# Casting v in its loading DMA, a PSUM bank for each pair of heads, and a new order: one core of Trainium2

## The chip, the cores and the metric

The kernel runs on one core of one Trainium2 chip. The metric is the device time of one execution in microseconds, taken as the median of several runs. A profile of one execution shows, for each instruction, its start and duration.

Names of the engines in the profile: PE is the matrix engine (PEld its weight loads), DVE the vector engine, ACT the scalar engine, POOL the GpSimd engine, SP the sync engine, which here only issues DMAs.

## The reference

The first half is linear attention with phi(x) = elu(x) + 1, over 8 batches, 8 heads, 576 positions and 64 values for each head. The second half is a multiplicative feed-forward network on the 4608 x 512 result.

```python
def phi(x):
    return np.where(x > 0, x, np.exp(x) - 1.0) + 1.0
q_p, k_p = phi(q), phi(k)
kv = einsum('bhsd,bhse->bhde', k_p, v)
z = sum(k_p, axis=2)
num = einsum('bhsd,bhde->bhse', q_p, kv)
den = einsum('bhsd,bhd->bhs', q_p, z)[..., None] + 1e-06
x = (num / den).transpose(0, 2, 1, 3).reshape(4608, 512)
a, b = x @ w1, x @ w2            # 512 x 1024 each
out = ((a * b) @ w3) @ w_out     # 1024 x 1024, then 1024 x 512
```

All inputs and the output are f32 in memory. The kernel computes its matmuls in bf16 and accumulates in f32.

## The kernel before, in words

The work is written as small steps. A string, `ORDER`, lists every step by name and arguments, and the program calls them in that order. Each engine executes its own instructions in the order in which the string issues them, and waits with semaphores for what it reads. So the order within one engine is fixed by hand, and only the waits between engines are left to run time. A second string, `GATES`, makes some loads wait for another load. SP and POOL issue DMAs in order, too: an issue that has to wait keeps all later ones on that engine back.

Of each batch the first 512 positions (128 partitions x 4, the index `j`) make chunk `b`. The last 64 positions of two batches share a tile (the "r" steps), and the eight remainders make chunk 8. `hp` is one of four pairs of heads.

Loading. `ld:n,b,h0,nh,queue` loads heads h0 to h0+nh of k, q or v of batch b as f32, one row of 1 KB for each head and partition; `lr` and `lp` load remainders; `lw`, `lo` and `l3` load w1 and w2, w_out and w3 with a cast to bf16 in the DMA, issued by POOL. `ld` tiles come from a pool of five buffers; a load waits until the tile five loads earlier is no longer read.

Feature map. `x` is exp on ACT, `t` is max(x, 0) + 1 on DVE, `m` the minimum of the two on DVE, which is phi; each `x` and `t` takes four heads, 1024 elements in a partition; each `m` before takes two heads, 512 elements. `xr`, `tr`, `mr` are the same for remainders.

Attention. `v` casts v into a tile `vt` with a column of ones beside each head, so that one product gives both kv and z; `vr` does so for the remainder. `kv` (batches 0 and 1) and `kk` (the others) are the products; `kc`, `kh` and `kg` copy them from PSUM to SBUF as bf16. `qt` and `qc` transpose phi(q) on PE and copy it (batches 0 and 1), `qd` does so by a DMA from SP (batches 2 to 7). `na` is phi(q) times kv for a pair of heads, `nd` the division on DVE (three instructions). `xp` and `xc` transpose the result on PE and copy it (chunks 0 to 2), `xd` does so by a DMA (chunks 3 to 7). `nar`, `ndr`, `qdr`, `xdr` are the remainder's.

Feed-forward. `w3t`, `w3c`, `wa`, `wf`, `wc` make w3 @ w_out once, so that the second half needs one product fewer. `f:c,f` gives 128 columns of a and of b for a chunk, 4 + 4 matmuls of 512 columns; it needs the transposed chunk `xt`. `ac` copies a from PSUM on ACT, `ab` multiplies it with b on DVE. `o:c,m` needs all eight `ab` of a chunk, 8 matmuls; `oc` copies the result and `st` stores it. `ol` is an `o` in two halves, the last of all. `warm` steps are matmuls on zeros.

PSUM has two pools: four buffers of one bank (`mm_ps`: w3, warm, qt, xp, a, b, o) and two of two banks (`at_ps`: wa, kv, kk, na, nar).

The lines that a sentence doesn't replace, the products of batches 0 and 1 (before):

```python
o = got(ps, ("kv", b), at_ps, [P, 2, 512], F32, "at", "kvp")
dst = o[:, g, a * PW:(a + 1) * PW]          # two pairs of heads in one bank
for j in range(NJ):
    nc.tensor.matmul(dst, kj[:, hp, j]..., vt[:, j, 2 * hp:2 * hp + 2, :]..., start=(j == 0), stop=False)
nc.tensor.matmul(dst, kr[...], vrz[...], start=False, stop=True)
```

Of the kernel before, what the change touches and what calls it, by code (L numbers as in the profile page):

```python
# [18 lines left out]
def kernel(  # L19
# [71 lines left out]


    @step
    def const(i):
        if i == 0:
            nc.vector.memset(zero, 0.0)  # L96
        elif i == 1:
            make_identity(nc, ident)
        elif i == 2:
            for t in vts:  # L100
                nc.vector.memset(t[:, :, :, D:E1], 1.0)
        elif i == 3:
            nc.vector.memset(vrz, 0.0)
            for s in range(2):
                nc.vector.memset(vrz[s * R:(s + 1) * R, s, :, D:E1], 1.0)
        else:
            nc.vector.memset(kvb[i - 4], 0.0)
# [8 lines left out]
    @step  # L116
    def ld_(n, b, h0, nh, queue):
        t = got(raw, (n, b), ld, [P, H * W], F32, "ld", f"{n}32")
        return queue_of[queue].dma_start(
            out=t[:, h0 * W:(h0 + nh) * W].rearrange("p (h x) -> p h x", x=W),  # L120
            in_=src[n][b, h0:h0 + nh, 0:NJ * P, :].rearrange("h (p j) d -> p h (j d)", j=NJ))

# [53 lines left out]
    @step  # L176
    def m(n, b, h0, hp):
        d = got(ph, (n, b), phi_p, [P, KC, NJ, 2, D], BF16, n)
        s = slice((2 * hp - h0) * W, (2 * hp - h0 + 2) * W)
        nc.vector.tensor_tensor(  # L180
            out=d[:, hp].rearrange("p j u d -> p u j d"),
            in0=ts[n, b, h0][:, s].rearrange("p (u j d) -> p u j d", u=2, j=NJ),
            in1=es[n, b, h0][:, s].rearrange("p (u j d) -> p u j d", u=2, j=NJ), op=ALU.min)
# [31 lines left out]
    @step  # L215
    def v_(b, h0, nh, eng):
        copy_of[eng](  # L217
            out=vts[b % len(vts)][:, :, h0:h0 + nh, 0:D],
            in_=raw["v", b].rearrange("p (h j d) -> p j h d", h=H, j=NJ)[:, :, h0:h0 + nh])

    @step
    def vr(b, eng):
        s = b % 2
        r = slice(s * R, (s + 1) * R)
        copy_of[eng](out=vrz[r, s, :, 0:D],
                     in_=raw["vr", b // 2][r].rearrange("p (h d) -> p h d", d=D))
# [3 lines left out]
    def kv(b, hp):  # L230
        o = got(ps, ("kv", b), at_ps, [P, 2, 512], F32, "at", "kvp")
        g, a = divmod(hp, 2)
        kj = ph["k", b]
        kr = ph["kr", b // 2, 2 if b > 1 else b]
        vt = vts[b % len(vts)]
        dst = o[:, g, a * PW:(a + 1) * PW]
        for j in range(NJ):
            nc.tensor.matmul(dst, kj[:, hp, j].rearrange("p u d -> p (u d)"),
                             vt[:, j, 2 * hp:2 * hp + 2, :].rearrange("p h e -> p (h e)"),
                             start=(j == 0), stop=False)  # L240
        nc.tensor.matmul(dst, kr[:, hp * P:(hp + 1) * P],
                         vrz[:, b % 2, 2 * hp:2 * hp + 2, :].rearrange("p h e -> p (h e)"),
                         start=False, stop=True)
# [4 lines left out]
    def kk(b, hp):  # L248
        o = got(ps, ("kk", b), at_ps, [P, 2, 512], F32, "at", "kvp")[:, 0]
        kj, kr, vt = ph["k", b], ph["kr", b // 2, 2], vts[b % len(vts)]  # L250
        for j in range(NJ + 1):
            for u in range(2):
                h = 2 * hp + u
                nc.tensor.matmul(o[u * D:(u + 1) * D, hp * E1:(hp + 1) * E1],  # L254
                                 kj[:, hp, j, u] if j < NJ else kr[:, h * D:(h + 1) * D],
                                 vt[:, j, h] if j < NJ else vrz[:, b % 2, h],
                                 start=(j == 0), stop=(j == NJ))

    @step
# [6 lines left out]
    def kc(b, g0, ng, r, eng):  # L266
        rows = slice(r * D, (r + 1) * D)
        copy_of[eng](  # L268
            out=kvb[b][rows, 2 * g0:2 * (g0 + ng), r, :].rearrange(
                "p (g a) e -> p g a e", a=2),  # L270
            in_=ps["kv", b][rows, g0:g0 + ng, 0:2 * PW].rearrange(
                "p g (a u e) -> p g a u e", a=2, u=2)[:, :, :, r, :])

    @step
    def kh(b, hp, r, eng):
        rows = slice(r * D, (r + 1) * D)
        g, a = divmod(hp, 2)
        c = a * PW + r * E1
        copy_of[eng](out=kvb[b][rows, hp, r, :], in_=ps["kv", b][rows, g, c:c + E1])

    @step
    def qt(b, h, n):
        t = ps["qt", b, h] = mm_ps.tile([P, NCH], F32, tag="mm", name="qtp").bitcast(
            BF16).rearrange("p (i t) -> p i t", t=P)
        for i in range(n):
            for j in range(NJ):
                nc.tensor.transpose(
                    t[:, i * NJ + j, :], ph["q", b][:, h + i, j].rearrange("p u d -> p (u d)"), ident)

    @step  # L290
    def qc(b, h, n, eng):
        d = got(sb, ("qt", b), att, [P, KC, NJ * P], BF16, "qt")
        copy_of[eng](out=d[:, h:h + n, :].rearrange("p i (j t) -> p (i j) t", t=P),
                     in_=ps["qt", b, h][:, 0:n * NJ, :])

    @step
    def qd(b):
        d = got(sb, ("qt", b), att, [P, KC, NJ * P], BF16, "qt")
        nc.sync.dma_start(out=d.rearrange("p c (j t) -> p (c j) t", t=P),
                          in_=ph["q", b].rearrange("p c j u d -> p (c j u d)"), transpose=True)  # L300
# [7 lines left out]
    def na(b, hp):  # L308
        o = ps["na", b, hp] = at_ps.tile([P, 2, 512], F32, tag="at", name="nd")
        for j in range(NJ):  # L310
            nc.tensor.matmul(o[:, j // 2, (j % 2) * 256:(j % 2) * 256 + PW],  # L311
                             sb["qt", b][:, hp, j * P:(j + 1) * P],
                             kvb[b][:, hp].rearrange("p u e -> p (u e)"),
                             start=True, stop=True)

    def divide(o, r, dst):
        nc.vector.tensor_scalar_add(out=r, in0=o[:, :, :, D], scalar1=1e-6)
        nc.vector.reciprocal(out=r, in_=r)  # L318
        nc.vector.tensor_tensor(  # L319
            out=dst, in0=o[:, :, :, 0:D],  # L320
# [3 lines left out]
    def nd(b, hp):  # L324
        x = got(sb, ("xn", b), att, [P, NJ, DM], BF16, "xn")
        r = small.tile([P, NJ, 2], F32, tag="r4", name="r")
        o = ps["na", b, hp].rearrange("p i (a x) -> p (i a) x", a=2)[:, :, 0:PW]
        divide(o.rearrange("p j (u e) -> p j u e", e=E1), r,
               x[:, :, hp * P:(hp + 1) * P].rearrange("p j (u e) -> p j u e", u=2))

    @step
    def nar(b):
        o = ps["nar", b] = at_ps.tile([P, 2, 512], F32, tag="at", name="ndr")
        for hp in range(KC):
            g, a = divmod(hp, 2)
            nc.tensor.matmul(o[:, g, a * PW:(a + 1) * PW], sb["qtr", b // 2][:, hp, :],  # L336
                             kvb[b][:, hp].rearrange("p u e -> p (u e)"),
# [3 lines left out]
    def ndr(b):  # L341
        x = got(sb, ("xnr", b // 2), att, [P, DM], BF16, "xnr")
        r = small.tile([P, 2, 4], F32, tag="r", name="r")
        w = slice((b % 2) * R, (b % 2 + 1) * R)
        divide(ps["nar", b][w, :, 0:2 * PW].rearrange("p g (a e) -> p g a e", e=E1), r[w],
               x[w].rearrange("p (g a e) -> p g a e", g=2, e=D))
# [93 lines left out]

    @step
    def o(c, m):
        d = ps["o", c, m] = mm_ps.tile([P, DM], F32, tag="mm", name="o_ps")
        for f in range(FC):
            nc.tensor.matmul(d, sb["ab", c][:, f, m * P:(m + 1) * P], wf_sb[:, f, :],  # L445
                             start=(f == 0), stop=(f == FC - 1))
# [32 lines left out]
    const:0 lr:k,0,s const:8 warm:26,0 warm:18,9 const:1 lr:v,0,s const:6 zr:0,1 l3:0 const:2 const:9  # L479
    l3:1 zr:0,0 const:11 l3:2 xr:k,0,0 tr:k,0,0 l3:3 const:5 lo:0,2 const:3 lo:2,2 lo:4,2 vr:0,a const:7  # L480
    w3t:0 const:10 lo:6,2 warm:8,1 w3c:0,v l3:4 mr:k,0,0 const:4 l3:5 w3t:1 warm:8,2 w3c:1,a
    ld:k,0,0,4,g w3t:2 warm:8,3 w3c:2,a ld:k,0,4,4,g w3t:3 warm:8,4 w3c:3,v ld:q,0,0,4,g wa:0,1 wa:1,1
    ld:q,0,4,4,g wa:2,1 ld:v,0,0,4,g wa:3,1 wa:4,1 ld:v,0,4,2,g wa:5,1 ld:v,0,6,2,g wa:6,1 wa:7,1 l3:6
# [106 lines left out]
```

## Time and profile before

| what | value |
|---|---|
| median of 3 runs | 251.77 us (251.26 to 253.02) |
| the profiled execution: its time | 251.52 us |
| the profiled execution: its span | 249.67 us |
| PE busy | 236.0 us |
| DVE busy | 164.1 us |
| ACT busy | 122.9 us |
| DMA | 50.10 MB, mean 201 GB/s |
| granted PE clock | 1.0 throughout |

How to read it: the span runs from the first to the last recorded event; the time of the execution holds some 1.85 us more around it. Busy times of different engines lie beside each other, so they don't add up to the span. A line of the timeline has start, duration, engine, line of the source, operation, output and inputs, shape and count, and in brackets the idle time of the engine before it with the instruction that ended it. A matmul's duration includes its way through the pipeline (about 0.16 us), so a row of eight of 512 columns shows 1.89 us although the next one can begin 1.73 us after the first.

### The profile page before, as it was taken

The numbers are of one execution on the slowest core, as the hardware profiler recorded it, in microseconds if no ns is written. First come the engines' busy times: TensorE is split into PE (matmuls) and PEld (weight loads), VectorE is DVE, ScalarE is ACT, GpSimd is POOL, SyncE is SP. The second block draws the span as 40 slices with busy tenths as digits, with TensorE's granted clock in tenths as the row PEclk, the third lists the DMA queues.
The fourth block names the chain that finished last, engine by engine and source line by source line (L and its number), as shares of the span: only waits on it lengthen the run. The fifth ranks groups of instructions, "written<-read, shape, count | busy, mean of one in ns | idle before, by whom it ended". The sixth has DMA issues, their size and how long they took to land.

```text
span 249.7 us, 4327 instructions
## 1 busy us (share of the span) xinstructions
PE 236.0 (95%) x1620; PEld 122.9 (49%) x1636; DVE 164.1 (66%) x364; ACT 122.9 (49%) x190; POOL 36.4 (15%) x59
## 2 busy tenths in 40 slices
PE   6897889979999989999999999999999999999994
PEld 6654844445444555454444454544544444444442
DVE  7518764977868999959649889786775365042320
ACT  3409554776956774665744835153352332323211
POOL 8554720001100210011000032200001100000000
PEclk9999999999999999999999999999999999999999
DMA  6999999999998999999999699975409511210155
GB/s 120 204 265 348 214 198 294 314 248 319 336 240 227 281 294 287 211 248 351 189 265 335 182 248 260 291 175 107 105 12 128 179 22 21 91 38 29 55 144 153
DMA packets 69621, 50.10 MB, mean 201 GB/s; under 512 B 41312, under 2 KB 64096, under 8 KB 69600
## 3 DMA queue, kind: packets, MB, share of 16 engines
q1 hardware_dynamic: 60416, 31.86, 54.1%
q0 software_dynamic: 9040, 17.83, 28.0%
q8 instruction: 13, 0.21, 0.3%
q10 hardware_dynamic: 144, 0.13, 0.2%
q14 instruction: 8, 0.07, 0.1%
HBM read 38.80 MB, written 9.44 MB: 193 GB/s over the span
## 4 chain that ended last, share of the span: by engine, by line
PE 56%; DMA 32%; DVE 4%; issue 3%; ACT 2%; POOL 1%; SPq 0%; ACTq 0%; POOLq 0%; DVEq 0%
PE a_ps L420 17%; PE o_ps L445 17%; PE b_ps L420 17%; DMA v<-in_v_dram 13%; DMA q<-in_q_dram 9%; DMA w_sb<-in_moe_w_dram 4%; DMA wo<-in_moe_w_out_dram 3%; DMA k<-in_k_dram 3%; DVE xn L319 2%; PE nd L311 2%; PE kvp L254 1%; POOL w3b L159 1%; PE ndr L336 1%; PE o_ps L472 1%; ACT vt L217 1%
## 5 line engine op out<-in xcount | busy, mean ns | idle before, releaser
L420 PEld LDWEIGHTS <-w_sb 128*128 128x128 bf16 x576 | 55.6, 98 | 64.6 <-issue 0.6
L439 DVE TENSOR_TENSOR ab<-a_sb,b_ps 128x512 bf16<-128x512 f32 x72 | 49.0, 684 | 43.7 <-PE b_ps L420 40.1
L434 ACT COPY a_sb<-a_ps 128x512 f32<-128x512 f32 x72 | 42.1, 584 | 58.8 <-PE a_ps L420 52.7
L420 PE MATMUL a_ps<-xt,w_sb 128*128 128x512 bf16 x256 | 66.0, 379 | 0.5 <-ACT xt L358 0.5
L420 PE MATMUL b_ps<-xt,w_sb 128*128 128x512 bf16 x256 | 66.0, 379 | 0.0
L445 PE MATMUL o_ps<-wf_sb,ab 128*128 128x512 bf16 x267 | 62.9, 379 | 1.0 <-issue 0.2
L445 PEld LDWEIGHTS <-ab 128*128 128x128 bf16 x280 | 26.4, 98 | 30.3 <-DVE ab L439 1.2
L463 POOL DMA_DIRECT2D out_dram<-o_sb x24 | 14.5, 605 | 148.7 <-ACT o_sb L451 130.9
L451 ACT COPY o_sb<-o_ps 128x512 f32<-128x512 f32 x24 | 14.0, 585 | 34.1 <-PE o_ps L445 31.9
L319 DVE TENSOR_TENSOR xn<-nd,r 128x512 bf16<-128x512 f32 x32 | 22.1, 692 | 1.1
L166 ACT ACTIVATE e<-q 128x1024 bf16<-128x1024 f32 x16 | 16.5, 1056 | 1.8 <-DMA q<-in_q_dram 1.8
L166 ACT ACTIVATE e<-k 128x1024 bf16<-128x1024 f32 x16 | 16.4, 1058 | 0.9 <-DMA k<-in_k_dram 0.8
L451 DVE COPY o_sb<-o_ps 128x512 f32<-128x512 f32 x11 | 7.6, 687 | 8.0 <-PE o_ps L445 8.0
L217 ACT CAST vt<-v 128x1024 bf16<-128x1024 f32 (+1 forms) x11 | 10.2, 933 | 5.4 <-PE kvp L254 2.7
L180 DVE TENSOR_TENSOR k<-t,e 128x512 bf16<-128x512 bf16 x32 | 12.2, 418 | 0.4 <-ACT e L166 0.2
L172 DVE TENSOR_SCALAR t<-q 128x1024 bf16<-128x1024 f32 x16 | 10.9, 688 | 2.1 <-DMA q<-in_q_dram 2.1
L180 DVE TENSOR_TENSOR q<-t,e 128x512 bf16<-128x512 bf16 x32 | 11.9, 420 | 0.2
L311 PE MATMUL nd<-kvb,qt 128*128 128x130 bf16 x128 | 10.9, 220 | 0.9 <-DVE kvb L268 0.4
L172 DVE TENSOR_SCALAR t<-k 128x1024 bf16<-128x1024 f32 x16 | 10.5, 688 | 1.2 <-DMA k<-in_k_dram 1.1
L311 PEld LDWEIGHTS <-qt 128*128 128x128 bf16 x128 | 8.7, 98 | 4.9 <-DVE xn L319 1.0
L113 PE MATMUL warm<-zero 128*128 128x128 bf16 x116 | 9.2, 241 | 1.2 <-DVE zero L96 1.2
L318 DVE RECIPROCAL r<-r 128x8 f32<-128x8 f32 (+1 forms) x40 | 8.1, 202 | 1.4
(76 smaller groups left out, 191.6 us busy)
## 6 DMA issues: line engine op xcount, KB each, us to landing
v<-in_v_dram SPq DMA_DIRECT2D x6, 1024.0 KB, 9.8
k<-in_k_dram SPq DMA_DIRECT2D x6, 1024.0 KB, 8.7
q<-in_q_dram SPq DMA_DIRECT2D x6, 1024.0 KB, 9.2
out_dram<-o_sb POOLq DMA_DIRECT2D x24, 256.0 KB, 6.1
w3b<-in_moe_w_dram POOLq DMA_DIRECT2D x8, 256.0 KB, 8.1
out_dram<-o_sb SPq DMA_DIRECT2D x7, 256.0 KB, 2.3
v<-in_v_dram POOLq DMA_DIRECT2D x3, 512.0 KB, 18.9
out_dram<-o_sb SPq DMA_DIRECT2D x9, 128.0 KB, 2.4
```

Source lines behind the costliest of these rows:

```text
L166: return nc.scalar.activation(out=e[:, 0:nh * W], in_=raw[n, b][:, h0 * W:(h0 + nh) * W], func=AF.Exp)
L172: nc.vector.tensor_scalar(out=d[:, 0:nh * W], in0=raw[n, b][:, h0 * W:(h0 + nh) * W], scalar1=0.0, scalar2=1.0, op0=ALU.max, op1=ALU.add)
L180: nc.vector.tensor_tensor(out=d[:, hp].rearrange("p j u d -> p u j d"), in0=ts[n, b, h0][:, s].rearrange("p (u j d) -> p u j d", u=2, j=NJ ...
L217: copy_of[eng](out=vts[b % len(vts)][:, :, h0:h0 + nh, 0:D], in_=raw["v", b].rearrange("p (h j d) -> p j h d", h=H, j=NJ)[:, :, h0:h0 + nh])
L311: nc.tensor.matmul(o[:, j // 2, (j % 2) * 256:(j % 2) * 256 + PW], sb["qt", b][:, hp, j * P:(j + 1) * P], kvb[b][:, hp].rearrange("p u e - ...
L319: nc.vector.tensor_tensor(out=dst, in0=o[:, :, :, 0:D], in1=r.unsqueeze(3).to_broadcast(list(r.shape) + [D]), op=ALU.mult)
L420: nc.tensor.matmul(o, w[:, kc, f * P:(f + 1) * P], xt_of(c)[:, :, kc, :], start=(kc == 0), stop=(kc == KC - 1))
L434: return copy_of[eng](out=d, in_=ps["a", c, f])
L439: nc.vector.tensor_mul(out=d[:, f, :], in0=sb["a", c, f], in1=ps["b", c, f])
L445: nc.tensor.matmul(d, sb["ab", c][:, f, m * P:(m + 1) * P], wf_sb[:, f, :], start=(f == 0), stop=(f == FC - 1))
L451: return copy_of[eng](out=d, in_=ps["o", c, m])
L463: queue_of[queue].dma_start(out=dst, in_=sb["o", c, m][r])
```

## The change

Four things are changed.

1. v of batches 0 and 1 (first 512 positions) is loaded by a new step `lv` on POOL, whose DMA casts to bf16. There is no `v` step for these batches. The product reads the loaded tile itself, which has no column of ones, so `kv` has for each `j` a second matmul of two columns against a small tile of ones.
2. Each pair of heads of `kv` has a PSUM bank of its own: a two-bank buffer for each two pairs. A tile of a pair is now laid out as one, head, head, one (`PW` = 130 columns), so that the two sums stand at its ends; `vt`, `vrz`, `kvb`, `na`, `nd`, `nar`, `ndr` and the copies follow this layout. For the batches 2 to 7 the cast `v` is divided by the head's place in its pair, `v:b,u`, and not by the half of the heads.
3. `m` takes four heads, 1024 elements, and phi's tile has the layout [P, NJ, H, D].
4. `ORDER` is another one, and so is the order of `GATES`. The new kernel also has the steps `kz`, `nt`, `ln`, `xm` and `o_part`; of these only `o_part` is used, by `o`. `const:12` sets the ones and two tiles that nothing reads.

```diff
+    ones = consts.tile([P, 2], BF16)
+    def of_pairs(t):
+        return t.rearrange("p j (c u) e -> p j c (u e)", u=2)
+    @step
+    def lv(b, h0, nh):
+        if ("vb", b) not in raw:
+            raw["vb", b] = ld.tile([P, H * W], F32, tag="ld", name="vb").bitcast(
+                BF16)[:, 0:H * W].rearrange("p (h j d) -> p h j d", h=H, j=NJ)
+        return nc.gpsimd.dma_start(
+            out=raw["vb", b][:, h0:h0 + nh].rearrange("p h j d -> p h (j d)"),
+            in_=v[b, h0:h0 + nh, 0:NJ * P, :].rearrange("h (p j) d -> p h (j d)", j=NJ))
     @step
-    def m(n, b, h0, hp):
-        d = got(ph, (n, b), phi_p, [P, KC, NJ, 2, D], BF16, n)
+    def m(n, b, h0, nh):
+        d = got(ph, (n, b), phi_p, [P, NJ, H, D], BF16, n)
...
     @step
-    def v_(b, h0, nh, eng):
+    def v_(b, u, eng):
         copy_of[eng](
-            out=vts[b % len(vts)][:, :, h0:h0 + nh, 0:D],
-            in_=raw["v", b].rearrange("p (h j d) -> p j h d", h=H, j=NJ)[:, :, h0:h0 + nh])
+            out=of_pairs(vts[b % len(vts)])[:, :, :, 1 + u * D:1 + (u + 1) * D],
+            in_=raw["v", b].rearrange("p (c u j d) -> p u j c d", u=2, j=NJ, d=D)[:, u])
     @step
     def kv(b, hp):
-        o = got(ps, ("kv", b), at_ps, [P, 2, 512], F32, "at", "kvp")
         g, a = divmod(hp, 2)
-        dst = o[:, g, a * PW:(a + 1) * PW]
+        dst = got(ps, ("kv", b, g), at_ps, [P, 2, 512], F32, "at", "kvp")[:, a, 0:PW]
         for j in range(NJ):
-            nc.tensor.matmul(dst, kj[:, hp, j].rearrange("p u d -> p (u d)"),
-                             vt[:, j, 2 * hp:2 * hp + 2, :].rearrange("p h e -> p (h e)"),
-                             start=(j == 0), stop=False)
+            k2 = of_pair(kj[:, j], hp)
+            nc.tensor.matmul(dst[:, 1:PW - 1].rearrange("p (u d) -> p u d", u=2), k2,
+                             vb[:, 2 * hp:2 * hp + 2, j], start=(j == 0),
+                             stop=False, skip_group_check=True)
+            nc.tensor.matmul(dst[:, 0:PW:PW - 1], k2, ones, start=False, stop=False, skip_group_check=True)
...
     def divide(o, r, dst):
-        nc.vector.tensor_scalar_add(out=r, in0=o[:, :, :, D], scalar1=1e-6)
+        nc.vector.tensor_scalar_add(out=r, in0=o[:, :, 0:PW:PW - 1], scalar1=1e-6)
...
```

The order, at the places that the prediction speaks of. First batch 0's products:

```diff
-    lw:0,1,256 x:q,0,4,4 m:q,0,0,0 warm:10,10 m:q,0,0,1 wc:4,v warm:10,11 m:k,0,4,2 qt:0,0,2 lw:1,1,256
-    v:0,0,4,v warm:10,12 t:q,0,4,4 lw:0,1,512 v:0,4,2,a kv:0,1 warm:10,13 m:q,0,4,3 lw:1,1,512 v:0,6,2,a
-    qc:0,0,2,v kv:0,2 kv:0,0 m:q,0,4,2 kh:0,2,1,a kv:0,3 kh:0,2,0,a kc:0,0,1,1,a kc:0,0,1,0,v qt:0,2,2
+    wf:5 m:q,0,0,4 lw:0,1,256 x:q,0,4,4 t:q,0,4,4 qt:0,0,2 wc:5,v warm:10,13 qc:0,0,2,a lw:1,1,256
+    m:q,0,4,4 kv:0,0 kv:0,1 lw:0,1,512 kv:0,2 kc:0,0,1,a kc:0,0,0,v kv:0,3 lw:1,1,512 kh:0,2,0,a
+    kh:0,2,1,v na:0,1 qt:0,2,2 kh:0,3,1,a kh:0,3,0,v ld:k,1,0,8,g nd:0,1 w3t:6 qc:0,2,2,a na:0,0 w3c:6,v
+    xp:0,1 w3t:7 nd:0,0 xc:0,1,a na:0,2 ld:q,1,0,8,g wf:6 lr:k,1,s w3c:7,v lv:1,0,4 lr:v,1,s nd:0,2
```

Then from chunk 1's o steps to chunk 2's f steps:

```diff
-    kk:2,1 kk:2,2 kk:2,3 v:3,0,4,v ld:q,4,0,8,s ab:1,5 o:1,1 kg:2,0,a kg:2,1,a v:3,4,4,v m:q,3,0,0
-    m:q,3,4,3 na:2,2 m:q,3,0,1 oc:1,1,a na:2,0 o:1,3 m:q,3,4,2 nd:2,0 st:1,1,g qd:3 nd:2,2 xp:2,0
-    oc:1,3,a o:1,0 t:k,3,4,4 vr:4,a st:1,3,g t:k,3,0,4 x:k,3,4,4 xp:2,2 x:k,3,0,4 na:2,3 m:k,3,4,2
-    na:2,1 m:k,3,4,3 o:1,2 nd:2,3 oc:1,0,a xc:2,2,a st:1,0,g m:k,3,0,0 xc:2,0,a nd:2,1 xp:2,3 x:q,4,0,4
-    m:k,3,0,1 xp:2,1 t:q,4,0,4 xc:2,3,a kk:3,0 kk:3,1 kk:3,2 kk:3,3 oc:1,2,v xc:2,1,a ld:v,4,0,8,s
-    kg:3,0,v st:1,2,g x:q,4,4,4 kg:3,1,v f:2,0 vr:5,v t:q,4,4,4 ac:2,0,a f:2,1 ab:2,0 ac:2,1,a m:q,4,4,2
+    x:q,3,0,4 f:1,5 ab:1,4 ld:k,4,0,8,s x:k,3,4,4 f:1,7 ac:1,5,a ab:1,5 ac:1,7,a lp:k,2,s ab:1,7 o:1,0
+    o:1,3 ld:q,4,0,8,s oc:1,0,a m:q,3,4,4 st:1,0,g m:q,3,0,4 x:k,3,0,4 t:k,3,4,4 qd:3 na:2,1 na:2,3
+    m:k,3,4,4 o:1,1 x:k,4,4,4 t:k,3,0,4 m:k,3,0,4 x:k,4,0,4 t:k,4,4,4 o:1,2 oc:1,1,a oc:1,3,v nd:2,1
+    st:1,1,g st:1,3,g oc:1,2,a t:k,4,0,4 na:2,0 xp:2,1 st:1,2,g nd:2,3 xr:k,2,2 xc:2,1,a ld:v,4,0,8,s
+    x:q,4,4,4 nd:2,0 na:2,2 xp:2,3 xc:2,3,a nd:2,2 kk:3 xp:2,0 tr:k,2,2 xp:2,2 lp:k,3,s kg:3,1,a
+    mr:k,2,2 xc:2,0,a xc:2,2,v m:k,4,0,4 f:2,1 kg:3,0,v m:k,4,4,4 ac:2,1,a t:q,4,0,4 x:q,4,0,4 f:2,4
```

SP's loads and transposes from batch 2 to the first load of batch 6, without the remainders, and the end of the order:

```diff
-    ld:v,2 ld:k,2 ld:q,2 ld:v,3 ld:q,3 qd:2 ld:k,3 ld:q,4 qd:3 ld:v,4 ld:k,4 qd:4 ld:k,5 xd:3 ld:q,5 ld:v,5 xd:4 qd:5 ld:v,6
+    ld:k,2 ld:v,2 ld:q,2 ld:v,3 ld:q,3 ld:k,3 qd:2 ld:k,4 ld:q,4 qd:3 ld:v,4 qd:4 xd:3 ld:q,5 ld:v,5 ld:k,5 ld:v,6 qd:5 xd:4
...
-    o:8,1 oc:8,3,a st:8,3,s o:8,0 oc:8,1,a st:8,1,s o:8,2 oc:8,0,v st:8,0,s o:7,0 oc:8,2,v st:8,2,s
-    oc:7,0,a st:7,0,s ol:7,3
+    st:8,2,s o:8,3 oc:8,1,v st:8,1,s o:8,0 oc:8,3,a st:8,3,s ol:7,3 oc:8,0,a st:8,0,s
```

At the start, POOL issues `l3:0` before the identity matrix is made (`const:1`); before it came after it.

## The prediction

> **What bounds the kernel now.** I read the page first (busy shares, slices), then the chain that ended last, then the timeline around each hole of PE. The page:
>
> ```profile
> PE 236.0 (95%) x1620; PEld 122.9 (49%) x1636; DVE 164.1 (66%) x364; ACT 122.9 (49%) x190; POOL 36.4 (15%) x59
> PE   6897889979999989999999999999999999999994
> DMA  6999999999998999999999699975409511210155
> ```
>
> PE is busy 95% of the span and nearly all its holes lie in the first 15 slices of 6.24 us. The DMA engines are full for about 25 slices. So only two things can pay: a shorter head, or fewer holes up to about 90 us. The chain shows who made these holes (start us, us, what):
>
> ```profile
> 32.68 19.71 DMA v<-in_v_dram
> 52.41 0.64 ACT vt L217
> ...
> 64.44 11.17 DMA q<-in_q_dram
> ...
> 76.88 7.36 DMA k<-in_k_dram
> ```
>
> The load of v of batch 1 lands at 52.41, and its cast for PE comes after that. The holes themselves, in the timeline (the bracket is the idle time before and its releaser):
>
> ```profile
> 36.36 0.38 PE L420 MATMUL a_ps<-xt,w_sb 128*128 128x512 bf16 x1 [0.45 <-ACT xt L358]
> ...
> 51.79 0.39 PE L238 MATMUL kvp<-vt,k 128*128 128x130 bf16 x4 [0.59 <-ACT vt L217]
> ...
> 53.09 0.39 PE L238 MATMUL kvp<-vt,k 128*128 128x130 bf16 x4 [0.58 <-ACT vt L217]
> ...
> 54.70 0.39 PE L238 MATMUL kvp<-vt,k 128*128 128x130 bf16 x4 [0.28 <-DVE kvb L279]
> ...
> 64.43 1.03 PE L420 MATMUL a_ps<-xt,w_sb 128*128 128x512 bf16 x4
> ...
> 79.09 1.92 PE L445 MATMUL o_ps<-wf_sb,ab 128*128 128x512 bf16 x7
> ...
> 88.70 0.40 PE L353 MATMUL xtp<-ident,xn 128*128 128x128 bf16 x4 [0.77 <-DVE xn L319]
> ...
> 89.79 1.04 PE L420 MATMUL a_ps<-xt,w_sb 128*128 128x512 bf16 x4
> ```
>
> The reader should take four marks from these: chunk 0's f steps end at about 51.0, chunk 1's begin at 64.43, chunk 1's o steps begin at 79.09, chunk 2's f steps begin at 89.79. After 89.79 PE runs to its last matmul at about 246.3 with holes of 0.5 us at most. The tail:
>
> ```profile
> 244.56 0.59 ACT L451 COPY o_sb<-o_ps 128x512 f32<-128x512 f32 x1 [4.59 <-PE o_ps L445]
> ...
> 246.35 0.37 ACT L474 COPY o_sb<-o_ps 128x256 f32<-128x256 f32 x1 [1.21 <-PE o_ps L472]
> 246.75 0.37 ACTq L476 DMA_DIRECT2D out_dram<-o_sb  x1
> ```
>
> The prices that I use, in us: f or o 8 x 0.216 = 1.73 of PE (four matmuls start 0.86 apart); one na, xp, or half a qt 0.22; kk 0.78; on DVE ab 0.69, t 0.65 (two take 1.29), nd 1.03 (60.25 to 61.29 from one to the next), xc 0.42; on ACT x 1.06, ac, oc and xc 0.59.
>
> **What the skill says.** "VectorE: DVE Perf Modes", section "The perf-mode tier table": tensor_tensor on bf16 in SBUF runs two elements a cycle, no more. The trace agrees (418 ns for 512, below one element a cycle), so the 1024-element minimum costs 418 ns plus another 512 at two a cycle, 267: 0.69 us. "DMA: Bandwidth & Descriptors", section "SWDGE vs HWDGE vs iDMA": only GpSimd's DMAs cast. Here every casting load is indeed on POOL's queue. "PSUM — Partial Sum Buffer", section "PSUM bank collisions": accesses by two engines must be kept apart by bank; the wait at 54.70, a kv behind copies from its bank, agrees. "TensorE: Matmul & The Clock Gate", section "Back-to-back issue gap": a matmul of up to 64 columns has a floor of about 25 ns; no row here has two columns.
>
> **The change, part by part.**
>
> Cast by DMA. Six casts of v go (on ACT three of 0.63 us and one of 1.04, on DVE 0.69 and 0.43). The number of POOL issues stays. The DMA view of the first 60 us, in slices of 1.5 us, has about 348 GB/s written where the f32 loads of k, q and v run (16 to 25 us), and about 200 GB/s of bf16 where casting loads run, which is 400 GB/s read: 1 MB takes 2.6 instead of 3.0 us. Two of them bring later loads 0.8 us forward, and l3:0 ahead of the identity on POOL perhaps 0.5 more.
>
> Ones matmuls. 8 kv steps x 4 = 32 more pairs of weight load and matmul. Ends: 25 ns (the skill's floor) and 57 ns (pitch of the 130-column pairs, (0.39-0.22)/3). I take 50 ns: 1.6 us of PE, 0.8 in each kv group. It is in the sums below; in batch 1 DVE is later than PE anyway, so it hides there, and costs 0.8 if DVE is not.
>
> Minimum over four heads. 64 x 0.419 becomes 32 x 0.69: 4.7 us less DVE over the span, spread out. On the critical DVE chains it counts 0.07 to 0.15 for each pair.
>
> Bank per pair. The 0.46 us wait in kv of batch 0 and the one at 54.70 go. But kv now takes both attention PSUM buffers, so na must wait for a group's copies; the order gives these first.
>
> Order. I followed the new queues engine by engine, each instruction starting at the later of its queue and its inputs.
>
> (a) Head to chunk 0's f. On DVE from 17.84 (end of wa): three copies, then t, m of k and q, bound by ACT's four exponentials between its copies, until m:q,0,4,4 ends at 27.0. The kv steps end on PE at 27.9, and na:0,1 starts there (29.60 before). DVE then has four nd, two w3c, and the xc: 28.3 + 4.1 + 1.3 + waits gives 33.9 and xt is complete at 35.4. Under it PE does both wf:6 and wf:7. Before, f work went on at 36.36 with wf:7 (1.73) still to do and 0.86 of f done, so it equals a start at 37.2. Gain 1.8. Eight f steps: 35.4 + 13.85 = 49.25, against 51.0.
>
> (b) Chunk 0's o, batch 1's attention. v1 is in by about 49.5, without cast, so no kv waits. DVE then has 15 operations and four nd in a row up to xc:1,2: t, t, m 2.0, ab and copies, m, t, m, four nd with four xc. With the waits on PE's na and on ACT it ends at about 63.0; xc:1,0 on ACT follows, and f:1,3 starts at 63.6 (64.43 before). Gain now 0.8.
>
> (c) f of chunk 1: 8 x 1.73 + kk 0.78 + one wait of 0.75 on ab:1,3 behind the minima: 79.0, against 79.09. Gain 0.1. The old order had f:1 running while DVE had less in front of ab.
>
> (d) Chunk 1's o to chunk 2's f. Here the new order queues on DVE, between ab:1,7 and f:2,1's last input xc:2,2: m:q3 twice, t and m of k3 twice, t:k4 twice, oc:1,3, four nd, tr, mr, xc. That is 4 x 0.69 + 4 x 0.65 + 0.68 + 4.12 + 3 x 0.42 = 11.4. ab:1,7 itself ends 1.3 after f:1,7 (its matmuls' tail, ab:1,5 ahead of it): 79.0 + 1.3 + 11.4 = 91.7. PE has only four o (6.92), four na, four xp and kk in the same time, 9.5. ACT is no earlier: x:q,4,4,4 sits before xc:2,3, kg:3,1 and xc:2,0, and q4, now behind k4 in SP's queue, lands at about 88.5 to 89.5; + 1.06 + 0.59 + 0.4 + 0.59 is 91 to 92. I take 91.6. The old order needed 10.7 for this stage, the new one 12.6. At the same remaining work PE stands 1.8 later than before.
>
> (e) From there to the last matmul nothing is left to win it back: PE had next to no holes. Both orders keep at least one f step (1.73) against about 1 us of DVE beside its ab. So + 1.8 there too.
>
> (f) Tail. ol's ACT copy now comes before oc:8,0 on ACT. After 246.72 + 1.8 come the issue 0.37, the copy 0.59, and two issues on SP of some 0.34, in place of the ACT issue alone: the last landing is 1.3 later.
>
> Sum: 1.8 + 1.3 = 3.1. The profiled execution took 251.52 (span 249.67 and 1.85 around it), which is 0.25 below the median of 251.77. So 251.52 + 3.1 = 254.6, 1.1% above the median. About 1% is what a measurement of this kernel can tell from no change.
>
> **Rivals.**
>
> 1. The head's gain is kept. Mechanism: DVE's chain in (d) is not the last to end; the point that decides is when f:2,1 starts: below 89.8 instead of 91.6. For it: DVE needs 4.7 us less, and v's cast and the bank waits, 2.3 us of holes from 51 to 55.3, are gone. Against it: the 11.4 us queue holds even when every load is early. Then f:2,1 starts 1.8 before the old mark (88.0), and the tail's 1.3 stays: 251.52 - 1.8 + 1.3 = 251.0, down to 249 where x:q,4 and the ones cost nothing.
>
> 2. Loads come late in the middle. q5, v5, k5 and v6 now stand behind xd:3 in SP's queue, while before k5 stood ahead of it. From v4's landing (about 97) to nd:3,1 (about 106) the DMA engines have little to do. xd:3 took 5.8, four loads at 3.75 follow, and x:q,5 sits on ACT ahead of ac:3,1. If q5 is 3.5 late, PE waits that long once its two f buffers are full: 258.1. Against it: kk:5 comes 6.8 us of PE work later than before.
>
> 3. It does not do what it says: the engines already do f32 and casting loads at one read rate, and the orders cost the same: 252.
>
> **How the numbers follow.** Forecast 0.45 (253.2 to 256.5: slower 0.35, within 1% 0.10); rival 1 0.33 (within 1% 0.23, faster 0.10); rival 2 0.17 (slower); rival 3 0.05 (within 1%). Sum: faster 0.10, within 0.38, slower 0.52. The range leaves the best of rival 1 and the worst of rival 2 out: 250.0 to 258.2.
>
> **What would show it.** Right: first f step of chunk 0 at 35 to 36, no ACT or DVE wait before the kv of batch 1, f:2,1 at 91 to 92 with idle before it from xt, DVE without idle from ab:1,7 to there, oc:8,0 after ol's copy in the tail. Wrong: f:2,1 below 90, or PE idle over 1 us behind e or a_sb after 110.

## The result, and the profile after

The changed kernel takes 255.56 us (median of 4 runs, 254.21 to 257.37), the kernel before on the same chip 252.06 (251.26 to 253.02). The ratio is 1.0142, with an interval of 1.0095 to 1.0189. The forecast was 254.6, slower by about 1.1%. The profiled execution, the shortest of the four, took 254.21 us with a span of 252.4, against 251.52 and 249.67 before: 2.7 us more. A ratio here and below is taken over the runs that lie within 1.5% of their kernel's fastest.

The page after (busy times, then PE and its granted clock in 40 slices of 6.31 us):

```profile
PE 237.8 (94%) x1668; PEld 124.6 (49%) x1668; DVE 163.8 (65%) x344; ACT 116.1 (46%) x178; POOL 34.1 (14%) x59
PE   8799899989799979999999999999999999999991
PEclk9999999999999999999999999999999999999997
```

ACT lost 6.8 us of work and DVE almost none of its sum. PE is full in every slice after the fifteenth but for the last one, which is nearly empty: the end is longer. (The lower clock in that slice lies behind PE's last matmul.) The marks of the prediction and the holes beside them, in PE's timeline after:

```profile
36.68 1.02 PE L471 MATMUL a_ps<-xt,w_sb 128*128 128x512 bf16 x4 [0.61 <-DVE xt L409]
...
54.13 1.04 PE L495 MATMUL o_ps<-wf_sb,ab 128*128 128x512 bf16 x4 [1.01 <-DVE ab L490]
...
64.31 0.40 PE L404 MATMUL xtp<-ident,xn 128*128 128x128 bf16 x4 [0.97 <-DVE xn L342]
65.43 1.02 PE L471 MATMUL a_ps<-xt,w_sb 128*128 128x512 bf16 x4 [0.72 <-ACT xt L409]
...
80.10 2.11 PE L495 MATMUL o_ps<-wf_sb,ab 128*128 128x512 bf16 x9
...
88.93 0.40 PE L334 MATMUL nd<-kvb,qt 128*128 128x130 bf16 x4 [0.86 <-DVE xn L342]
89.97 0.32 PE L282 MATMUL kvp<-vt,k 128*64 128x65 bf16 x8 [0.41 <-DVE xn L342]
91.86 1.02 PE L471 MATMUL a_ps<-xt,w_sb 128*128 128x512 bf16 x4 [0.47 <-ACT xt L409]
```

No kv of batch 1 waits for a cast any more. In place of those waits stand a hole at 54.13, two at 64 to 65 and three at 89 to 92, all behind DVE's or ACT's queue. The hole at 54.13 begins on ACT (first line; the second is the vector engine's `ab` behind it):

```profile
45.73 0.62 ACT L248 CAST vrz<-v32r 64x512 bf16<-64x512 f32 x1 [2.22 <-DMA v32r<-in_v_dram]
...
46.99 0.69 DVE L490 TENSOR_TENSOR ab<-a_sb,b_ps 128x512 bf16<-128x512 f32 x1 [2.44 <-ACT a_sb L485]
```

The new order put `vr:1`, the cast of the v remainder, on ACT. It waits 2.22 us for its load with the last four `ac` copies of chunk 0 behind it; `ab` is late, and `o` waits for `ab`. The last microseconds, all engines:

```profile
246.56 0.34 SPq L534 DMA_DIRECT2D out_dram<-o_sb  x1
247.03 0.37 ACT L532 COPY o_sb<-o_ps 128x256 f32<-128x256 f32 x1 [2.93 <-PE o_ps L530]
247.43 0.37 ACTq L534 DMA_DIRECT2D out_dram<-o_sb  x1
247.90 0.59 ACT L509 COPY o_sb<-o_ps 128x512 f32<-128x512 f32 x1 [0.49 <-ACT o_sb L532]
248.51 1.10 SPq L521 DMA_DIRECT2D out_dram<-o_sb  x2
```

`oc:8,0` (L509) now follows `ol`'s copy (L532), and two stores are issued after it. Before, the issue at 246.75 was the last event of this kind.

Busy times in stretches show where PE gained and lost (length; then PE, PEld, DVE, ACT and POOL busy with their counts, PE clock, DMA share, GB/s). Before:

```profile
52.00:66.00 14.00, 12.66 (x106) 7.53 (x105) 10.55 (x27) 10.70 (x20) 1.93 (x4) 1.00 1.12 312
80.00:92.00 12.00, 11.18 (x111) 6.12 (x111) 11.54 (x30) 8.62 (x13) 2.59 (x4) 1.00 1.12 286
92.00:247.00 155.00, 153.11 (x934) 74.48 (x941) 97.92 (x215) 65.99 (x103) 9.73 (x16) 1.00 0.68 169
```

After:

```profile
52.00:66.00 14.00, 11.30 (x99) 6.56 (x96) 11.60 (x30) 8.96 (x15) 2.20 (x4) 1.00 1.11 319
80.00:92.00 12.00, 10.27 (x107) 5.79 (x105) 11.11 (x25) 8.03 (x13) 2.23 (x4) 1.00 1.17 250
92.00:247.00 155.00, 154.95 (x952) 75.28 (x950) 99.69 (x202) 64.55 (x101) 8.73 (x16) 1.00 0.65 164
```

From 52 to 66 and from 80 to 92 PE does 2.3 us less than before; from 92 on it does 1.8 more and is full. Of these 1.8 us, 0.7 lie behind the last matmul of the kernel before, which began at 246.00.

### The profile page after: what moved, and what is told of

It reads as the page before. It is cut to its first block, busy times and chain, and to the rows that moved or that the text cites. A ratio compares the mean times of both kernels' runs of the same rounds, so it can differ in the third digit from the quotient of the medians.

```text
span 252.4 us, 4363 instructions
## 1 busy us (share of the span) xinstructions
PE 237.8 (94%) x1668; PEld 124.6 (49%) x1668; DVE 163.8 (65%) x344; ACT 116.1 (46%) x178; POOL 34.1 (14%) x59
## 4 chain that ended last, share of the span: by engine, by line
PE 81%; DVE 7%; ACT 4%; DMA 3%; issue 2%; POOL 1%; ACTq 0%; DVEq 0%; POOLq 0%
PE a_ps L471 24%; PE b_ps L471 24%; PE o_ps L495 21%; DMA wo<-in_moe_w_out_dram 3%; PE wa L444 3%; PE nd L334 2%; DVE t L196 2%; PE kvp L282 2%; PE wf_ps L459 1%; DVE xn L342 1%; DVE ab L490 1%; DVE k L203 1%; DVE q L203 1%; ACT e L190 1%; PE ndr L387 1%
## 5 line engine op out<-in xcount | busy, mean ns | idle before, releaser
L495 PE MATMUL o_ps<-wf_sb,ab 128*128 128x512 bf16 x280 | 64.2, 379 | 1.0 <-DVE ab L490 1.0
L521 POOL DMA_DIRECT2D out_dram<-o_sb x24 | 13.2, 549 | 137.7 <-ACT o_sb L509 120.6
L509 ACT COPY o_sb<-o_ps 128x512 f32<-128x512 f32 x22 | 12.9, 586 | 40.7 <-PE o_ps L495 40.1
L509 DVE COPY o_sb<-o_ps 128x512 f32<-128x512 f32 x13 | 8.9, 686 | 9.5 <-PE o_ps L495 9.5
L203 DVE TENSOR_TENSOR k<-t,e 128x1024 bf16<-128x1024 bf16 x16 | 10.9, 689 | 1.6 <-ACT e L190 0.9
L203 DVE TENSOR_TENSOR q<-t,e 128x1024 bf16<-128x1024 bf16 x16 | 10.8, 686 | 0.5
L128 PE MATMUL warm<-zero 128*128 128x128 bf16 x116 | 9.9, 255 | 1.2 <-DVE zero L107 1.2
L196 DVE TENSOR_SCALAR t<-k 128x1024 bf16<-128x1024 f32 x16 | 10.7, 687 | 0.0
L128 PEld LDWEIGHTS <-zero 128*128 128x128 bf16 x116 | 9.0, 118 | 1.4 <-DVE zero L107 1.2
```

Of the source, the lines that this page charges most:

```text
L128: nc.tensor.matmul(t[:, 0:P], zero[:, 0:P], zero[:, 0:P], start=True, stop=True)
L196: nc.vector.tensor_scalar(out=d[:, 0:nh * W], in0=raw[n, b][:, h0 * W:(h0 + nh) * W], scalar1=0.0, scalar2=1.0, op0=ALU.max, op1=ALU.add)
L203: nc.vector.tensor_tensor(out=d[:, :, h0:h0 + nh].rearrange("p j h d -> p h j d"), in0=ts[n, b, h0][:, 0:nh * W].rearrange("p (h j d) -> p ...
L509: return copy_of[eng](out=d, in_=ps["o", c, m])
L521: queue_of[queue].dma_start(out=dst, in_=sb["o", c, m][r])
```

## The experiments

The theory was that the order costs the time and the parts (casting load, ones products, a bank for each pair, minimum over four heads) do not. The rival was the reverse. All ratios are to the kernel before, run beside it on the same chip.

### The old order with the new parts

```diff
-    ORDER = (the changed kernel's)
+    ORDER = (that of before; v of batches 0 and 1 as lv, no v step for them, one m for each two)
```

> The changed kernel with all its parts (v of batches 0 and 1 cast by its load, ones products, a bank per pair of heads, minimum over four heads), but with the order list of the kernel before, translated: the two minima of a pair stand as one where the second stood, the casts of v of batches 0 and 1 are dropped. Theory 1, the loss is in the new order (vector queue ahead of the third chunk's f, ol's copy ahead of the last output copy, the v remainder's cast on the scalar engine, the head's l3:0): 250.5 to 252.5 us, a ratio to before of 0.995 to 1.003, chunk 2's f at about 90, and the end after the last matmul shorter by about 2 than in the changed kernel. Theory 2, the loss is in the parts (casting loads, ones products, two kv buffers) and the order is neutral: 254 us or more, ratio 1.01 or above.

Measured: 251.07 us, ratio 0.9982 (0.9965 to 0.9998), span 249.6. The marks are those of before to 0.05 us (64.39, 79.05, 89.77), and so is the end:

```profile
246.31 0.37 ACT L532 COPY o_sb<-o_ps 128x256 f32<-128x256 f32 x1 [1.21 <-PE o_ps L530]
246.71 0.37 ACTq L534 DMA_DIRECT2D out_dram<-o_sb  x1
```

So under the old order all parts together cost nothing (they gain 0.2%), and the loss comes with the new order. This run decides the main question.

### The tail alone

```diff
-  ... ol:7,3 oc:8,0,a st:8,0,s
+  ... oc:8,0,a st:8,0,s ol:7,3
```

> The changed kernel with one entry of the order moved: the last ol:7,3 stands behind the store st:8,0, so that the copy oc:8,0 comes before ol's copy on the scalar engine, as in the kernel before. Theory 1: the last store's issue comes back by about 2 us and the time falls by 1.5 to 2.1, to 253.4 to 254.1 (ratio to before 1.006). Theory 2, the end is set by the other stores or by their landing: less than 0.5 us, 255 or more.

Measured: 253.79 us, ratio 1.0073 (1.0045 to 1.0101). The last `o` matmul began at the same time as in the changed kernel (246.67), and the span is 250.9 instead of 252.4:

```profile
245.28 0.58 ACT L509 COPY o_sb<-o_ps 128x512 f32<-128x512 f32 x1 [1.19 <-PE o_ps L495]
...
246.99 0.37 ACT L532 COPY o_sb<-o_ps 128x256 f32<-128x256 f32 x1 [1.12 <-PE o_ps L530]
247.09 0.54 SPq L534 DMA_DIRECT2D out_dram<-o_sb  x1
247.39 0.37 ACTq L534 DMA_DIRECT2D out_dram<-o_sb  x1
```

The profiles put the tail at 1.5 us, the ratios at 0.7%, about half of the loss. The tail is still 0.6 us longer than before (4.25 us from the start of the last matmul to the end of the span, against 3.67): the first half of `ol` was copied by 246.54, but its store on SP stands behind five others and is issued at 247.09.

### Parts taken out of the new order

v loaded as f32 and cast again, without ones products:

```diff
-  lv:0,0,4 ... kv:0,0 ... lv:1,0,4 ... kv:1,0
+  ld:v,0,0,4,g ... v:0,0,a v:0,1,v kv:0,0 ... ld:v,1,0,4,g ... v:1,0,a v:1,1,v kv:1,0
```

> The changed kernel with v of batches 0 and 1 loaded as 32-bit floats again and cast on the scalar and vector engines just ahead of the first kv of its batch, and without the ones products (kv reads the cast v with its ones columns); the bank per pair, the minimum over four heads and the order stay. Theory 1, the casting load is by itself neutral to helpful (it saves a wait of about 1.4 us ahead of batch 1's kv and costs 0.9 us of ones products): 255 to 257, that is 0 to 1.5 us slower than the changed kernel. Theory 2, the part costs more than it saves: 254 or less.

Measured: 257.90 us, ratio 1.0245 (1.0200 to 1.0290), above the range of either theory. In its trace the first kv of batch 0 waits 1.5 us and that of batch 1 2.3 us for the cast `vt`. Theory 2 falls. How much is the cast and how much the place that I gave it, last ahead of kv, this run doesn't tell; in its profile, too, the load of `vr:1` landed late (47.38), and PE ran at half clock from 54.43 to 57.84.

Without the ones products:

```diff
-            nc.tensor.matmul(dst[:, 0:PW:PW - 1], k2, ones, start=False, stop=False, skip_group_check=True)
```

> The changed kernel without the 64 ones products of batches 0 and 1 (it leaves out z of the first 512 positions of these batches; nothing else moves). Each was 27 ns in the changed kernel's trace (83 ns for a pair of products), so 0.9 us for the 32 ahead of each chunk. Theory 1: they are on the path in both chunks, but a wait for k or phi takes their place in part: 0.3 to 1.5 us less than the changed kernel, 254.1 to 255.3 (ratio to before 1.008 to 1.013). Theory 2, they are the loss: 2.5 us or more, 253 or less.

Measured: 255.42 us, ratio 1.0137 (1.0082 to 1.0192): no difference that can be told from the changed kernel. The expectation has twice as many of them as there are: the trace shows 32 ones matmuls, 16 for each batch, so they come to 0.4 us ahead of each chunk and not 0.9. Their own price is read in the changed kernel's trace, a product and its ones matmul in turn, 80 ns from one product to the next:

```profile
51.09 0.17 PE L267 MATMUL kvp<-ones,k 128*128 128x2 bf16 x1
51.11 0.22 PE L264 MATMUL kvp<-vb,k 128*128 128x128 bf16 x1
51.17 0.17 PE L267 MATMUL kvp<-ones,k 128*128 128x2 bf16 x1
51.19 0.22 PE L264 MATMUL kvp<-vb,k 128*128 128x128 bf16 x1
```

The minimum over two heads instead of four:

```diff
+        for h in range(0, nh, 2):
             nc.vector.tensor_tensor(... 512 elements instead of 1024)
```

> The changed kernel with each minimum over four heads as two over two heads, as in the kernel before, at the same place: the vector engine gets 32 more instructions of 0.42 us in place of 0.69 each pair's, 0.15 us more for each minimum, 4.7 us in all. Theory 1: in the stretch ahead of chunk 2's f, where the vector engine has no idle time, four minima make it 0.6 us later; elsewhere it is hidden: 0.3 to 1.2 us above the changed kernel, ratio to before 1.014 to 1.020. Rival, it is hidden there too: ratio as the changed kernel's within its error, f of chunk 2 no later than 92.0 where chunk 1's o starts at 80.1.

Measured: 257.00 us, ratio 1.0196 (1.0142 to 1.0251), inside theory 1's range, but its interval overlaps the changed kernel's. DVE is busy 166.1 us instead of 163.8: 2.3 us more, where the expectation and the prediction had counted 4.7 from the durations of single minima, which overlap (16 pairs of k alone come to 12.0 us, 0.75 for a pair, not 0.84). Chunk 1's o to chunk 2's f takes 12.03 us instead of 11.76. In the same execution `vr:1` waited longer, and chunk 1's o was already 2.4 us late, so its 257 is not the minimum's price alone:

```profile
47.92 0.62 ACT L249 CAST vrz<-v32r 64x512 bf16<-64x512 f32 x1 [4.18 <-DMA v32r<-in_v_dram]
```

The bank for each pair was not taken out alone.

### The wait of vr:1

```diff
-  f:0,3 ac:0,0,a ab:0,0 ac:0,3,a vr:1,a f:0,7 ab:0,3 ac:0,7,a ... kv:1,0 ac:0,4,a kv:1,1
+  f:0,3 ac:0,0,a ab:0,0 ac:0,3,a f:0,7 ab:0,3 ac:0,7,a ... kv:1,0 ac:0,4,a vr:1,a kv:1,1
```

The tail is mended here too. Since kv:1,0 now stands ahead of vr:1, the first pair of heads of batch 1 is computed without its remainder of v.

> The changed kernel with two entries of the order moved: the last ol:7,3 behind st:8,0 (as before), and the cast of batch 1's v remainder, vr:1 on the scalar engine, behind ac:0,4 instead of ahead of ac:0,7. In the profiled runs so far this remainder landed between 43.9 and 48.2 us with the same order ahead of it, and the scalar engine's copies of chunk 0 stood behind it. Theory 1: the holes of chunk 0's f and first o (0.4 and 1.1 us with the tail alone, up to 2.2 and 3.4 us of half clock in another run) go, the time falls by 0.5 to 2 us below the run with the tail alone (1.0073) to a ratio of 0.999 to 1.005, and its runs lie closer together than the 3 us of the changed kernel. Rival, chunk 1's f is held by something later all the same (it has a hole of 1.1 and one of 0.9 at 64 to 65): no change, 1.006 or above.

Measured: 253.01 us, ratio 1.0047 (1.0027 to 1.0066). Of its 22 runs 19 lie from 252.1 to 254.8, three at 256.2 to 257.7. The holes of chunk 0 went, and chunk 1's f began at 64.58 instead of 65.43. Against the tail alone that is 0.3% better, with overlapping intervals: likely, not shown. The profiled execution then lost most of it again:

```profile
64.58 1.16 PE L471 MATMUL a_ps<-xt,w_sb 128*128 128x512 bf16 x4 [0.67 <-ACT xt L409]
65.53 1.91 PE L471 MATMUL b_ps<-xt,w_sb 128*128 128x512 bf16 x4
67.24 1.78 PE L471 MATMUL a_ps<-xt,w_sb 128*128 128x512 bf16 x4
68.85 1.03 PE L471 MATMUL b_ps<-xt,w_sb 128*128 128x512 bf16 x4
```

Four matmuls take 1.71 us from start to start (65.53 to 67.24) where they take 0.87 a little later: PE's clock was halved for 3.4 us (65.34 to 68.75), a loss of about 1.6. The Trainium skill, "TensorE: Matmul & The Clock Gate", section "What's actually happening", says that PE falls to half its clock after an idle window of about 3.4 us, and that the window runs freely. The length agrees, the idle window doesn't: here PE was busy for 1.69 of the 3.41 us just ahead, with two holes of 0.97 and 0.67 us and four small matmuls between them, at the place where the changed kernel has nearly the same two holes and stayed at full clock in its profile. The last section comes back to this.

### The third stage

```diff
-  ... m:k,3,0,4 x:k,4,0,4 t:k,4,4,4 o:1,2 oc:1,1,a oc:1,3,v nd:2,1 ... nd:2,3 ... nd:2,0 ... nd:2,2
+  na:2,1 na:2,3 nd:2,1 nd:2,3 ... na:2,0 na:2,2 ... nd:2,0 nd:2,2 xc:2,1,a xc:2,3,a x:k,4,0,4 t:k,4,4,4 o:1,2 ...
```

> The changed kernel with only the stretch between na:2,1 and f:2,1 of the order written anew: the four nd steps and their copies stand ahead of the key group of batch 4 on the vector engine, and the query step x:q,4,4 behind xc:2,2. Theory 1, the vector queue makes the third chunk late and nothing later wins it back: f of chunk 2 starts at 89.5 to 90.5 instead of 91.9, and the time falls by 1.2 to 2.2 us to 253.3 to 254.4. Rival, the gain is absorbed by what follows (batch 4's phi come later and their users wait, or slack up to the end): f of chunk 2 starts earlier, but the time falls by less than 0.7 us, or rises.

Measured: 256.35 us, ratio 1.0181 (1.0141 to 1.0222): no gain. Half the clock struck from 65.86 to 69.27 here, too, so chunk 1's o began 1.5 us later. But the stage itself became longer: chunk 2's f stopped after two matmuls, since the copy xc:2,2 now stood on DVE behind two t of k4 and oc:1,3.

```profile
93.07 0.59 PE L471 MATMUL a_ps<-xt,w_sb 128*128 128x512 bf16 x2 [0.90 <-ACT xt L409]
94.75 0.59 PE L471 MATMUL a_ps<-xt,w_sb 128*128 128x512 bf16 x2 [1.09 <-DVE xt L409]
```

My edit moved DVE's queue ahead of another input of the same f; it doesn't speak for or against the step.

### Orders grafted together

With the tail mended, a stretch of the old order was set into the new one. Old up to chunk 2's o, new from there:

> All parts of the change; the order of the kernel before up to chunk 2's first o, the order of the changed kernel from there on, and the last ol:7,3 behind st:8,0. Theory 1, three separate stretches of the new order differ: up to chunk 2's o the old one is 2.9 us ahead (o of chunk 2 starts at 104.5 against 107.4), after it the new one needs 139.2 to its last matmul against 141.4. Then the two gains add: last matmul at about 243.7, time 2.9 below the run with only the tail moved: ratio to before 0.993 to 0.998. Rival, the new order is quicker at the end only because it comes late there (its transfers and phi are a fixed time ahead): the gain is absorbed and the last matmul stays at 245.6 or later, ratio 1.002 or above.

Old up to chunk 1's o only:

> All parts of the change; the order of the kernel before up to chunk 1's first o, then that of the changed kernel, with the last ol:7,3 behind st:8,0. Theory 1: chunk 1's o starts at 79.1 instead of 80.1, chunk 2's f at 90.8 instead of 91.9, and the whole is 1.0 shorter than with the tail alone: ratio 1.001 to 1.005. Rival, the vector queue of the third stage holds f of chunk 2 at 91.9 whatever comes before: no gain, ratio 1.006 or above.

Old only from chunk 1's o to chunk 2's o:

> All parts of the change; the changed kernel's order, but between chunk 1's first o and chunk 2's first o the order of the kernel before, and the last ol:7,3 behind st:8,0. Theory 1, the third stage is what the vector queue makes long: from chunk 1's o to chunk 2's f 10.7 us instead of 11.8, to chunk 2's o 25.5 instead of 27.3, and 1.9 less than with the tail alone: ratio 0.998 to 1.003. Rival, the stage is as long in either order because k of batch 4 and the copies have to be done anyway: less than 0.5 gained, ratio 1.005 or above.

Measured: ratios 1.0067 (1.0028 to 1.0105), 1.0261 (1.0214 to 1.0308) and 1.0281 (1.0232 to 1.0331). The twelve runs of the first spread from 252.33 to 258.55 us, with a median of 255.89. None came out as theory 1 had it. All three ratios lie in their rivals' ranges, but not for the rivals' reasons. In the first, the old part ran as expected (chunk 1's f at 63.61, chunk 2's at 88.99), and a seam at kk:4 took it back, a wait of 1.78 us for a phi of k that the new order makes earlier, with one of 1.14 us behind it. In the second, `t` of k4 waited 4.16 us on DVE for its load, with `nd` behind it:

```profile
92.06 0.62 PE L334 MATMUL nd<-kvb,qt 128*128 128x130 bf16 x4 [6.25 <-DVE xn L342]
```

PE was at half clock from 89.69 to 99.93 there. In the third, vr:1 met a late load (48.22), PE stood for 2.05 us and ran at half clock for 3.4 us after it; kk:4's seam came on top. So these runs price seams, not stages: an order's compute steps and its loads belong together.

Old up to chunk 3's f, where the two orders have about the same work behind them:

> All parts of the change; the order of the kernel before up to chunk 3's first f, the order of the changed kernel after it, vr:6 behind ab:3,5 and the last ol:7,3 behind st:8,0. In the run with the order to chunk 2's o a seam of two holes (1.95 and 1.3 us, kk:4 placed ahead of what it needs) ate 3 us; this cut has no such seam. Theory 1: chunk 3's f starts at 113 to 114 with 2.2 us more work done by then than in the changed kernel, and from there the new order needs about 1 us less: last matmul at 244 to 245, ratio to before 0.991 to 0.997. Rival, the later half is the same in either order: last matmul near 246, ratio 0.998 to 1.001.

Measured: 251.71 us, ratio 0.9981 (0.9953 to 1.0009). The time is the rival's, that of the old order throughout, but not for the rival's reason: the last matmul began at 245.20, 0.75 earlier than in the run with the old order (245.95), of which 0.3 was there at chunk 3's f. The span is only 0.2 shorter (249.4), since the tail of the new order, mended as it is, took 4.24 us from there on and that of the old order 3.67. In this profile the new order is 0.4 us quicker for PE after chunk 3's f, and the tail takes that back.

### Four places mended at once

```diff
-  vr:1,a ... xc:1,1,v oc:0,1,a xp:1,2 nd:1,0 v:2,0,a ... xp:1,0 ... (third stage) ... ol:7,3 oc:8,0,a
+  vr:1,v ... na:1,0 ... nd:1,2 ... nd:1,0 ... xc:1,1,v xp:1,0 xc:1,0,a ... v:2,0,a ... (nd ahead of t:k,4) ... oc:8,0,a st:8,0,s ol:7,3
```

> The changed kernel's order with its four late places mended, parts untouched: vr:1 on the vector engine behind ab:0,5; na:1,0 and nd:1,0 ahead of the copies xc:1,1 and xc:1,2, with m:k,2,4 and v:2,0 behind them; in the third stage the four nd steps ahead of the phi of batch 4's k, which moves behind xc:2,2; and the last ol:7,3 behind st:8,0. Theory 1, these four waits are the loss: chunk 1's kv starts at about 50.6, its f at 63 (65.4 in the changed kernel), chunk 2's f at 87 to 88.5 (91.9), and the end follows: 3 to 4 us below the run with only the tail moved, ratio to before 0.988 to 0.997. Rival, what is won early is given back, since batch 4's phi and the transfers come at their own time (new holes in chunk 2's f and at kk:4): ratio 0.998 to 1.006, with the last matmul at 245.5 or later.

Measured: 256.10 us, ratio 1.0131 (1.0077 to 1.0186). Chunk 1's f began at 64.08 and chunk 2's at 91.26. The ratio lies above both ranges. As the rival had it, what was won early was given back; in the profiled execution, the longest of the six (257.84 us), the place is a load:

```profile
82.77 7.28 SPq L322 DMA_TRANSPOSE qt<-q  x1
90.14 0.54 SPq L134 DMA_DIRECT2D v<-in_v_dram  x1
...
101.93 1.07 ACT L240 CAST vt<-v 128x1024 bf16<-128x1024 f32 x1 [5.57 <-DMA v<-in_v_dram]
...
103.53 1.28 PE L471 MATMUL b_ps<-xt,w_sb 128*128 128x512 bf16 x4 [3.55 <-ACT a_sb L485]
```

On SP the load of v4 stands behind the transposition of batch 3's q. That took 7.28 us here and 5.03 in the changed kernel, so v4 was issued at 90.14 instead of 87.45, its cast held the `ac` copies of chunk 2, and half clock followed (104.15 to 107.56). Whether the shorter runs met the same wait isn't shown: two of them took 253.51 and 254.22, the other three 256.03 to 256.83.

## Why the prediction was right

The sum was 3.1 us on one profiled execution, and the profiles show 2.7: 0.7 at the last matmul and 2.0 in the tail. The forecast's mechanism, a new order that pays on the vector queue and on the tail, is what the old order's run confirms. But its terms were off in both directions and met in the middle; that the sum came out so near is luck.

(a) predicted chunk 0's f at 35.4, and it came at 36.68: of the gain of 1.8 only 0.5. I had given l3:0 ahead of the identity perhaps 0.5 of gain; `wa` in fact began at 11.98 instead of 11.16. Whether l3:0 did that isn't shown: in four runs with the old head order `wa` began at 11.41, 12.28, 12.28 and 13.30. What the casting loads themselves gained, 0.8 us by the prediction, no run tells apart.

(b) predicted 63.6 for chunk 1's f; measured 65.43. That kv of batch 1 would not wait for a cast was right, and in this profile it doesn't wait for the load either (with the tail alone it did, 0.91 us). What failed is the queue that I followed: the wait of vr:1 on ACT was not in it, nor did I see that nd:1,0 stands directly before xp:1,0 with only four transpositions on PE to cover it. That left the holes of 1.01, 0.97 and 0.72.

(c) predicted 15.4 us for chunk 1's f stage with one wait of 0.75; it took 14.67 without that wait. The mark was 80.10 instead of 79.0.

(d) predicted 91.6 for chunk 2's f; measured 91.86. The queue of 11.4 us between ab:1,7 and xc:2,2 is there: DVE is never idle for more than 0.1 us between the start of ab:1,7 at 80.37 and that of xc:2,2 at 91.73. This was the best step. f itself did not wait for xc:2,2, which its third matmul reads, but for the copy xc:2,0 on ACT (line at 91.86). That copy's transposition stands on PE behind kk:3, which waits for DVE's third division (line at 89.97). The stage took 11.76 us (10.7 in the old order, with old and new parts alike) rather than 12.6: ab:1,7 ended 0.96 after chunk 1's o had begun and not 1.3, the queue took 11.1, and its last copy ended after f had begun. q4 was no limit.

(e) predicted that nothing is won back: this step failed. From chunk 2's f to the last matmul PE needed 154.8 us instead of 156.2, so the 2.1 us by which it started late shrank to 0.7. The work is the same: 952 matmuls in the changed kernel and in the run with the old order, which needed 156.2, too (the trace before lists 942, since some records are missing). So the old order lost 1.4 us more to small waits there, six of 0.18 to 0.27 us in that run, and I called them next to nothing.

(f) predicted 1.3 for the tail; measured 2.05 (2.73 more in the span, less the 0.68 by which ol's copy came later), and 1.5 by the run with only the tail moved. The mechanism is shown; of the missing 0.75, the two issues on SP took 1.10 instead of 0.68, oc:8,0 began 0.49 after ol's copy and not the 0.37 of the issue between them, and the rest, about 0.2, came after the last issue.

The ones products were priced at 50 ns and took about 25 (80 ns for a pair, of which the product takes 55, the pace of eight transpositions of 128 columns in a row): the lower end, the floor that the Trainium skill gives in "TensorE: Matmul & The Clock Gate", section "Back-to-back issue gap". The minimum at 0.69 us was met (689 ns), but not the 4.7 us that it was to save on DVE: about half of that. Rival 2, late loads in the middle, did not occur in the changed kernel but did in the last experiment, by v4 and not by q5.

Open: the median is 1.35 us above the profiled run, and the run with only the tail moved leaves 0.7%. One part is the wait of vr:1, whose load landed between 43.9 and 48.2 us over the profiles. In three profiles with the same order up to there it landed at 45.73, 46.84 and 47.92, and chunk 1's f began at 65.43, 66.43 and 67.84 (changed kernel, without ones, minimum over two heads). Where it landed earlier (44.84 and 43.94), chunk 1's f came at 65.43 and 65.22, behind other waits. Another is half clock. The record has each run's mean granted clock, and 3.4 us at half clock lower it by 0.007. In the run with vr:1 and the tail moved, eight runs have a mean clock of 0.987 to 0.993 and a median of 254.5 us, the other fourteen 0.996 or more and 252.7. But half clock isn't all: the changed kernel's run of 256.46 us has 0.997, which leaves room for about 0.8 us by this estimate. How the loss divides among these parts, and the holes ahead of chunk 1's f, is not shown.

## What to carry to other kernels

Test an edit that comes with a new order by running its parts under the old order first: one run told parts from order, where eight edits of the order told far less. On an engine that executes in order, a step that waits for a load belongs behind everything that is due sooner, and the last store's chain must not stand behind another. Small holes over a long stretch add up; sum them before saying that nothing can be won back there.

## What was not expected of the hardware

- Half clock. Seven of the profiles have a stretch of it ahead of PE's last matmul: 3.41 us long in six, 10.24, three times that, in the seventh (behind the hole of 6.25 us). In each profile the changes of the clock lie whole multiples of 3.41 us apart, in steps whose place differs between executions. In the step at full clock just ahead of half clock PE was busy for 1.72 of the 3.41 us or less. After a step at full clock with 1.76 us or more the clock was never halved; between 1.52 and 1.72 it was or it wasn't. So the same two holes can cost 1.6 us or nothing. The third-stage run has both in one step (first line, the half clock after it in the second), the changed kernel has a border of two steps between them (last two lines; after the length come PE, PEld, DVE, ACT and POOL busy, then the clock):

```profile
62.45:65.86 3.41, 1.72 (x17) 0.93 (x15) 3.24 (x9) 2.67 (x4) 0.54 (x1) 1.00 1.06 338
65.86:69.27 3.41, 3.41 (x10) 1.21 (x9) 3.27 (x7) 2.59 (x3) 0.00 (x0) 0.50 1.06 338
...
61.27:64.68 3.41, 2.44 (x22) 1.43 (x21) 3.27 (x11) 3.02 (x5) 1.08 (x2) 1.00 1.06 310
64.68:68.10 3.42, 2.70 (x14) 1.24 (x13) 3.28 (x7) 2.26 (x5) 0.00 (x0) 1.00 1.08 358
```

- The landing time of one 128 KB load, the v remainder of batch 1, moved by 4.3 us between executions.
- The DMA transposition of q of batches 2 and 3 took from 3.1 to 7.6 us on SP's queue, and every later load on SP waited behind it.
